# A branch hint as TensorE's first instruction, in place of a visit to a stop inside its loop

## The chip, the cores and the metric

The kernel runs on one core of one Trainium2 chip. The metric is device time in microseconds (us), taken over several executions; lower is better. For every profiled execution there are a page, groups, chains and timelines, and the trace's records of single DMA packets.

Names: PE is TensorE, PEld its weight loads, DVE is VectorE, ACT is ScalarE, POOL is GpSimd, SP is SyncE, which issues nearly all loads. The core has 16 DMA engines, and all loads but that of x are split over all of them (45 loads, each with 16 closing packets of 4 bytes in the trace of the kernel before).

## The reference, cut to what matters

It is one decode step for two sequences: attention over a long cache, a small MLP beside it, and a gate.

```python
xn = layernorm(x)                       # x: 2 x 1 x 512, bf16
q = xn @ wq                             # 512 x 4096: 32 heads of 128
p = softmax(q @ k_cache.T / sqrt(128))  # 8 kv heads, 32768 positions, 2 sequences
s = (p @ v_cache) @ wo                  # 4096 x 512
g = silu(mlp(xn))                       # w3: 512 x 1792, w4: 1792 x 512
return x + s * g
```

The two caches hold 268 of the 280.5 MB that the kernel reads. Each byte is used once, so reading them is most of the work.

## The kernel before: the parts that matter

SP issues the load of wq as its very first instruction, ahead of the three barriers at the start. The other loads follow. TensorE runs a loop of 16 passes, one per (sequence, kv head), after a prologue and before a tail.

The change concerns how TensorE's program itself comes onto the core. The trace of the kernel before has one packet of 16 KB of kind "instruction" among the loads (queue q8, at 4.354 us); its transfer is called the fetch below. The author took it for a later part of TensorE's program; that is an estimate, and e2 and f2 below show what supports it. Before, TensorE was sent at the start through a short stop inside its loop (the "visit", at 0.69 us), so that the packet would be asked for early:

```python
def begin(nc, ins, engine, far):
    ...
    entry.instructions = head + [ins, mybir.InstUnconditionalBranch(target=far, ...)]
    ...                                       # the rest of the entry block goes to "far_back"

first = sp.dma_start(out=wq_t[...], in_=A_wq...)           # 4 MB, first of all loads
begin(nc, first.ins, pe.engine, "far")
...
hint_p, hint_v = pe.mark_branch_hint_location(), dve.mark_branch_hint_location()
...
with pe.Fori(0, NG):                          # 16 passes
    head_sums()
    ...                                       # 64 score matmuls
    nc.br("mid", engines=[pe.engine])         # each pass jumps over the stop:
    with nc.body("far", ...):
        pe.sem_inc(s_far, 1)
        nc.br("far_back", engines=[pe.engine])
    nc.switch_bb("mid")
    ...                                       # 64 p @ v matmuls
early(0); head_sums(); early(1); product(2)   # the tail: s @ wo, part by part as wo lands
...
for i in range(3, len(WO_PARTS)):
    mm = product(i)
...
for eng, hint, reg in ((pe, hint_p, end_p), (dve, hint_v, end_v)):
    eng.br_lt(reg, 1, on_true="fin", on_false="end").branch_hint(hint)   # "the end hint"
```

The softmax here doesn't subtract the row's maximum and nothing guards it: scores larger than these inputs give would overflow.

## Time and profile before

| | before |
|---|---|
| time, median of 3 runs | 654.35 us (654.28 to 654.38) |
| span of the profiled run | 652.9 us |
| read from HBM | 280.50 MB, 430 GB/s over the span |
| PE, DVE busy | 60%, 53% |
| first load issued / next load issued | 0.00 / 1.97 us |
| last wo packet ends | 649.92 us |

The first lines are from the page of the kernel before: the DMA row (busy tenths in 40 slices of the span) and the DMA queues (packets, MB, share of 16 engines' time).

```profile
span 652.9 us, 6540 instructions
...
DMA  9999999999999999999999999999999999989997
...
q1 hardware_dynamic: 6492, 280.50, 99.4%
q8 instruction: 1, 0.02, 0.0%
...
q14 instruction: 1, 0.01, 0.0%
```

DMA is the limit from end to end. The small line to notice is q8: one packet of 16 KB that carries instructions, not data.

The second view is the end of the chain of waits of the kernel before (start us, length us, what).

```profile
613.26 36.95 DMA kbuf<-in_A_wo_dram
650.22 0.04 issue
650.26 0.26 PE bank L643 x4
650.52 0.02 issue
650.54 0.30 DVE sg L667
650.85 0.02 issue
650.87 0.29 DVE out L669
```

The kernel ends less than 3 us after the last piece of wo has landed. So a delay of the DMA engine that delivers last should delay the kernel (in f2 below wo landed 1.1 us earlier, and the span was 1.0 us shorter).

The third view is the start of the timeline of the kernel before (start us, length us, engine, line, operation).

```profile
0.00 0.39 SPq L182 DMA_DIRECT2D kbuf<-in_A_wq_dram  x1
...
1.97 0.33 SPq L225 DMA_DIRECT2D vbuf<-in_B_w_dram  x1
...
2.27 0.27 DVE L254 MEMSET x_bf<- 128x256 uint32 x1 [2.27 <-PEq L187]
```

The packet records show one thing that no view shows. On one DMA engine a packet starts where the packet before it ends (to some nanoseconds: 1655 + 1478 is 3133, and the next starts at 3131), so the records can be chained by engine. On the engine that carries the instruction packet, with start and length in ns:

```
kernel before, one DMA engine:   1655 +1478  wq, 32 KB
                                 3131 +1224  wq
                                 4354  +925  instructions, 16 KB (q8)
                                 5264 +1720  wq
                                 6981 +1219  wq ...
```

The others need about 1213 ns for a wq packet from the fourth on. This engine loses 910 ns to the fetch (5264 - 4354) and 507 ns to the slower packet behind it (1720 - 1213), 1.4 us together. It ends its share of wq at 13.04 us; the next latest ends at 12.11. At the end of the kernel one engine is late again: its last wo packet ends at 649.92 us, the next latest engine's at 648.90. (The 8 KB instruction packet on q14, which ends at 648.98, belongs to no load and isn't counted.) The lag can be followed in between: each load ends on each engine with a packet of 4 bytes, 16 for a load, and in every load up to 640 us the last of the 16 is behind the one before it by 0.93 us at first and 1.02 us from about 290 us on.

### The profile page before, as it was taken

What the parts mean: (1) busy time and instruction counts of PE and PEld (TensorE: products, weight loads), DVE (VectorE), ACT (ScalarE), POOL (GpSimd) and SP (SyncE); (2) the same over time, 40 slices, a digit from 0 to 9 for tenths busy, and PEclk for the clock granted to TensorE, in tenths of its full rate; (3) what the DMA queues carried; (4) which work ended last, traced back from release to release, by engine and by line L of the source; (5) the groups of instructions that cost most, each with busy time, mean ns of one, the idle gap of its engine ahead of it and who ended that gap; (6) DMA issues with size and microseconds to landing.
All of it is one profiled execution on the core that took longest, in us unless ns stands there. A gap on an engine that the chain in (4) does not pass through costs nothing. (4 is left out here: it accounts for less than half of the span.)

```text
span 652.9 us, 6540 instructions
## 1 busy us (share of the span) xinstructions
PE 390.0 (60%) x2406; PEld 156.8 (24%) x2438; DVE 345.8 (53%) x412; ACT 76.8 (12%) x184; POOL 7.7 (1%) x29
## 2 busy tenths in 40 slices
PE   0548195672828658293764829367383945828785
PEld 0213132221313223131221213123121322312332
DVE  3257191744809265391835729174481926539570
ACT  1320102011010200101020010201001020110100
POOL 2100000000000000000000000000000000000000
PEclk9769788786978868698786978878697896869797
DMA  9999999999999999999999999999999999989997
GB/s 384 477 391 452 446 446 401 442 446 450 401 438 446 450 406 434 446 450 401 438 446 450 418 422 450 446 430 410 450 446 442 397 450 446 450 389 448 418 450 292
DMA packets 6506, 280.53 MB, mean 430 GB/s; under 512 B 736, under 2 KB 1000, under 8 KB 1256
## 3 DMA queue, kind: packets, MB, share of 16 engines
q1 hardware_dynamic: 6492, 280.50, 99.4%
q8 instruction: 1, 0.02, 0.0%
q10 hardware_dynamic: 12, 0.01, 0.0%
q14 instruction: 1, 0.01, 0.0%
HBM read 280.50 MB, written 0.00 MB: 430 GB/s over the span
## 5 line engine op out<-in xcount | busy, mean ns | idle before, releaser
L586 PE MATMUL bank<-T,z 128*128 128x512 bf16 x992 | 272.9, 422 | 185.1 <-PEq L46 180.4
L513 DVE STREAM_TRANSPOSE T<-kbuf 128x1024 int32<-128x1024 int32 x256 | 290.6, 1210 | 126.3 <-DVEq L46 126.3
L586 PEld LDWEIGHTS bank<-T,z 128*128 128x128 bf16 x1024 | 97.4, 103 | 347.9 <-issue 270.3
L608 PE MATMUL bank<-vbuf,pt 128*16 128x512 bf16 x1024 | 77.5, 469 | 2.9 <-PEq L46 2.9
L490 ACT ACTIVATE ep<-bank 128x512 bf16<-128x512 f32 x32 | 19.1, 598 | 434.2 <-ACTq L46 434.2
L534 DVE RECIPROCAL rec<-bank 128x1 f32<-128x1 f32 (+1 forms) x17 | 2.9, 169 | 123.1 <-DVEq L46 123.1
L608 PEld LDWEIGHTS bank<-vbuf,pt 128*16 128x16 bf16 x1024 | 28.6, 105 | 43.6 <-issue 28.0
L522 DVE STREAM_TRANSPOSE pt<-ep 128x512 bf16<-128x512 bf16 x32 | 22.8, 714 | 22.1 <-DVEq L46 22.1
L568 PE MATMUL bank<-ob,sel_o 128*128 128x128 f32 x136 | 19.4, 286 | 16.4 <-PEq L46 16.4
L601 PE MATMUL bank<-ones_f,sm 128*128 128x1 f32 x32 | 5.9, 255 | 31.3 <-PEq L46 31.3
L494 ACT COPY ob<-bank 128x512 f32<-128x512 f32 x16 | 9.4, 587 | 107.2 <-ACTq L46 107.2
L568 PEld LDWEIGHTS bank<-ob,sel_o 128*128 128x128 f32 x136 | 16.7, 193 | 21.8 <-issue 21.8
L483 ACT ACT_TABLE_LOAD x16 | 20.5, 1283 | 0.3
L483 ACT COPY z<-qr 32x16 bf16 x64 | 13.0, 203 | 0.7
L601 PEld LDWEIGHTS bank<-ones_f,sm 128*128 128x128 f32 x32 | 5.0, 198 | 32.2 <-issue 32.2
L329 PE MATMUL bank<-ident,xn_bf 17*128 17x17 bf16 x4 | 0.3, 176 | 14.1 <-POOL x L320 14.1
L452 PE MATMUL bank<-vbuf,h_bf 128*32 128x512 bf16 x14 | 4.6, 501 | 6.4 <-DVE h_bf L449 6.4
L563 PE MATMUL bank<-ident 128*1 128x1 bf16 x64 | 8.4, 165 | 0.0
L563 PEld LDWEIGHTS bank<-ident 128*1 128x1 bf16 x64 | 4.0, 82 | 16.2 <-issue 14.4
L542 DVE TENSOR_REDUCE oA<-xm 128x128 f32 x16 | 5.9, 366 | 3.8 <-DVEq L46 3.8
L536 DVE SCALAR_TENSOR_TENSOR xm<-bank,rec,mask 128x128 f32<-128x128 f32 (+1 forms) x17 | 6.0, 351 | 2.5 <-DVEq L46 0.2
L490 ACT ACTIVATION_READ_ACCUMULATOR ep<-bank 128x1 f32 x32 | 6.4, 200 | 0.2
(75 smaller groups left out, 54.9 us busy)
## 6 DMA issues: line engine op xcount, KB each, us to landing
vbuf<-in_A_v_cache_dram SPq DMA_DIRECT2D x4, 4096.0 KB, 29.1
kbuf<-in_A_k_cache_dram SPq DMA_DIRECT2D x2, 4096.0 KB, 22.9
kbuf<-in_A_wq_dram SPq DMA_DIRECT2D x1, 4096.0 KB, 13.5
vbuf<-in_B_w_dram SPq DMA_DIRECT2D x2, 1792.0 KB, 17.7
kbuf<-in_A_wo_dram SPq DMA_DIRECT2D x3, 1024.0 KB, 34.3
kbuf<-in_A_wo_dram SPq DMA_DIRECT2D x1, 512.0 KB, 37.1
kbuf<-in_A_wo_dram SPq DMA_DIRECT2D x1, 256.0 KB, 37.3
kbuf<-in_A_wo_dram SPq DMA_DIRECT2D x2, 128.0 KB, 37.0
```

The costliest lines, as they stand in the source:

```text
L483: i = act.copy(out=z[32 * j:32 * j + 32, :, :, c:c + rep], in_=qr[32 * j:32 * j + 32, :, :, bass.ds(m * rep, rep)],)
L490: act.activation(out=eps_[i][:, :], in_=sc[i][:, :], func=ACT.Exp, scale=inv_sqrt_dh, accum_out=rss[i][:, :]).then_inc(s_e, 1)
L494: act.copy(out=ob[:, :], in_=o[:, :]).then_inc(s_ob, 1)
L513: dve.transpose(out=Ts[(NR * i + r) % T_BUFS][:, :].rearrange("p (b t k) -> p t b k", b=NB, t=RT), in_=kt[:, r * W:(r + 1) * W].rearrange( ...
L522: dve.transpose(out=pts[h][:, :, :].rearrange("p r (t h) -> p t r h", h=rep), in_=eps_[i][:, :].rearrange("p (t r h) -> p t r h", r=NR, h= ...
L536: dve.scalar_tensor_tensor(out=xm[p0:, :, :], in0=oT[p0:, :].rearrange("p (w r) -> p w r", w=WL), scalar=rec[p0:, 0:1], in1=mask[p0:, :].u ...
L542: dve.tensor_reduce(out=dst, in_=xm[p0:, :, :].rearrange("p w r -> p r w"), axis=AX.X, op=ALU.add).then_inc(s_r, 1)
L563: pe.matmul(mark_ps, lhsT=ident[:, 0:1], rhs=ident[:, 0:1], start=True, stop=True).then_inc(sem, 1)
L568: mm = pe.matmul(oT, lhsT=sel_o[:, t, :, :, :].rearrange("p j h w -> p (j h w)"), rhs=ob[:, t * Dh:(t + 1) * Dh], start=(t == 0), stop=(t ...
L586: mm = pe.matmul(sc[i][:, :], lhsT=z[:, nb, e, zc:zc + 128], rhs=Tb[:, nb, :, e], start=(r == 0 and nb == 0 and e == 0), stop=(r == NR - 1 ...
L601: pe.matmul(S, lhsT=sms[1][:, :], rhs=ones_f[:, 0:1], start=True, stop=True)
L608: mm = pe.matmul(o[32 * j:32 * j + VT * rep, :], lhsT=pts[h][:, r, a * VT * rep:(a + 1) * VT * rep], rhs=vt[:, u * VT:(u + 1) * VT, :].rea ...
```

## The change

The intent is to get the packet early without a detour: TensorE need not go to the stop and come back while the first barrier waits for it (TensorE's DRAIN comes at 1.08 us, SP's at 0.455), and the loop loses the jump over the stop. A branch at the top, never taken, has a target in the tail ("late"), and a hint that it will be taken is moved to be TensorE's first instruction.

```diff
-def begin(nc, ins, engine, far):
+def begin(nc, *names):            # now only moves the named instructions to the top
...
-    begin(nc, first.ins, pe.engine, "far")
...
+    ahead = pe.mark_branch_hint_location()
+    top = nc.cur_bb
+    pe.br_lt(end_p, 0, on_true="late", on_false="go").branch_hint(ahead)   # end_p is 0
+    nc.switch_bb("go")
     hint_p, hint_v = pe.mark_branch_hint_location(), dve.mark_branch_hint_location()
+    hints = [i.name for i in top.bb.instructions if isinstance(i, mybir.InstBranchHint)]
+    begin(nc, first.ins.name, *hints)
...
-        nc.br("mid", engines=[pe.engine])
-        with nc.body("far", parent=nc.bb_map["main"], valid_engines=[pe.engine]):
-            pe.sem_inc(s_far, 1)
-            nc.br("far_back", engines=[pe.engine])
-        nc.switch_bb("mid")
...
+    nc.switch_bb("late", parent=top)
     for i in range(3, len(WO_PARTS)):
```

More of the change, by code (lines that the diff above doesn't have):

```diff
@@ L46, in take @@
     eng.wait_ge(sem, n).then_inc(sem, -n)
-def begin(nc, ins, engine, far):
+def begin(nc, *names):
     blocks = nc.m.functions[0].blocks
+    moved = [i for b in blocks for i in b.instructions if i.name in names]
     for b in blocks:
-        b.instructions = [i for i in b.instructions if i.name != ins.name]
-    entry = blocks[0]
-    at = next(n for n, i in enumerate(entry.instructions) if isinstance(i, (mybir.InstMemset, mybir.InstDrain)))
-    head, rest = entry.instructions[:at], entry.instructions[at:]
-    entry.instructions = head + [ins, mybir.InstUnconditionalBranch(target=far, name=f"I-{nc.next_id()}", engine=engine)]
-    with nc.body(f"{far}_back", parent=nc.bb_map[blocks[0].name]):
-        pass
-    *blocks, back = nc.m.functions[0].blocks
-    back.instructions = rest
-    nc.m.functions[0].blocks = blocks[:1] + [back] + blocks[1:]
+        b.instructions = [i for i in b.instructions if i.name not in names]
+    entry = blocks[0].instructions
+    at = next(n for n, i in enumerate(entry) if isinstance(i, (mybir.InstMemset, mybir.InstDrain)))
+    blocks[0].instructions = entry[:at] + moved + entry[at:]
 @with_exitstack
@@ L191 @@
         eng.reg_mov(reg, 0)
+    s_far = nc.alloc_semaphore("s_far")
+    ahead = pe.mark_branch_hint_location()
+    top = nc.cur_bb
+    pe.br_lt(end_p, 0, on_true="late", on_false="go").branch_hint(ahead)
+    nc.switch_bb("go")
     hint_p, hint_v = pe.mark_branch_hint_location(), dve.mark_branch_hint_location()
-    s_far = nc.alloc_semaphore("s_far")
+    hints = [i.name for i in top.bb.instructions if isinstance(i, mybir.InstBranchHint)]
+    begin(nc, first.ins.name, *hints)
     d_x, d_w3, d_w4 = (Count(nc, n) for n in ("d_x", "d_w3", "d_w4"))
```

## The prediction

The sum of the forecast is 654.3 us less 0.7, so 653.6 us. The first step of point 1, on which the 0.7 us rest: the packet, asked for at 0.7 us (the visit) or 2.2 us (the hint) before, would be asked for at about 0.1 to 0.5 us. That a hint is such a request was the assumption. "It" in point 1 is this request; before that, in "It found wq's packets", it is the packet.

> **What bounds the kernel now.** DMA. The page shows the DMA row at 9 tenths in nearly every slice, queue q1 at 99.4% of 16 engines' span, 430 GB/s; PE is 60% busy. The chain that ended last is 5.7% "DMA kbuf<-in_A_wo", 36.95 us of waiting that ends at 650.22, then 0.26 us of PE, 0.30 + 0.29 us of DVE and the output DMA. So the time is 280.5 MB through the DMA engine that finishes last, plus a short tail.
>
> **The engine that finishes last.** I chained the trace's packet records (a packet starts where the one before it on its engine ends). One of the 16 DMA engines is late. It carries a 16,384-byte packet of kind "instruction" (queue q8 on the page: one packet, 0.02 MB), which starts at 4.35 us, takes 0.925 us and is followed by a wq packet of 1.72 us where the others take 1.21: about 1.4 us lost. This engine ends its share of wq at 13.03 us, the next latest at 12.10, most at 11.5 to 11.9. At the end of the kernel 15 engines finish wo by 648.90 and one at 649.91. Every load is split evenly over the engines, so a lag of about 1.0 us from the instruction fetch stays to the end, all on the critical path.
>
> The compiled program before has about 662 TensorE instructions. [...] It found wq's packets (from 1.66 us on this engine) ahead of it.
>
> **What the change does.**
> 1. [...] If it reaches its DMA engine before wq's first packet there (1.66 us), it runs in idle time and the lag shrinks from 1.0 us to about 0.0 to 0.3. If it arrives behind that packet, it costs about what it costs now.
> 2. No visit: TensorE reaches its first DRAIN at about 0.2 us instead of 1.08; the first barrier then waits for SP's DRAIN (0.455), so the three barriers end about 0.5 us earlier (now 1.9 us, timeline). That is off the path: wq is issued at 0.00 before them and keeps the engines busy to 11.5 us.
> 3. The branch over the far block goes (estimate 0.2 us x16 on PE, by the 0.23 us from the branch back to the next instruction). Off the path: PE waits for data in every group.
>
> **Predicted.** 653.6 us, 0.7 us less: about 70% for a gain of 0.5 to 1.0 us, 25% for none, little for worse. Range 653.2 to 654.5. Within 2%: nearly certain.
>
> **What the profile would show.** The q8 packet before or among wq's first packets, at about 1 to 2 us; the same count (one) of them; the engine that carries it no later than the others at the end of wq (about 12.1 us); the last wo packet at about 649.0 instead of 649.91, and landing at about 649.3; first SP issue after the barrier at about 1.4 instead of 1.97 us.
>
> **What would make it wrong.** The fetch still lands behind wq packets (then 654.3); the hint at the first instruction is ignored[...]; other engines' lag (12.10 at wq's end) limits the gain to less; a second fetch appears[...].

## The result, and the profile after

| | before | after |
|---|---|---|
| time, median of 6 runs each | 654.37 us (654.28 to 654.43) | 654.42 us (654.16 to 654.63) |
| span of the profiled run | 652.9 us | 652.8 us |
| next load issued | 1.97 us | 1.45 us |
| instruction packet q8 starts | 4.354 us | 5.578 us |
| latest / next latest engine at the end of wq | 13.04 / 12.11 us | 13.05 / 12.17 us |
| latest / next latest engine at the end of wo | 649.92 / 648.90 us | 649.84 / 648.96 us |

The ratio of the times is 1.0001, with a 95% interval of 0.9988 to 1.0013: no difference. Ratios here and below are the mean time of one kernel's fast runs over that of the other's of the same rounds, so not quite the ratio of the medians quoted beside them.

The page of the changed kernel has the same queues, with the same single instruction packet on q8.

```profile
span 652.8 us, 6524 instructions
...
DMA  9999999999999999999999999999999999999997
...
q1 hardware_dynamic: 6492, 280.50, 99.4%
q8 instruction: 1, 0.02, 0.0%
...
q14 instruction: 1, 0.01, 0.0%
```

The end of its chain of waits has the same form, and the same times within 0.1 us:

```profile
613.16 36.97 DMA kbuf<-in_A_wo_dram
650.13 0.04 issue
650.18 0.26 PE bank L637 x4
650.44 0.02 issue
650.46 0.30 DVE sg L662
650.76 0.02 issue
650.79 0.29 DVE out L664
```

The start of its timeline shows that the barriers do end earlier:

```profile
0.00 0.39 SPq L176 DMA_DIRECT2D kbuf<-in_A_wq_dram  x1
...
1.45 0.33 SPq L224 DMA_DIRECT2D vbuf<-in_B_w_dram  x1
...
1.75 0.27 DVE L253 MEMSET x_bf<- 128x256 uint32 x1 [1.75 <-PEq L181]
```

So the 0.52 us at the start is there, and nothing comes of it. The fetch, which was to come earlier, comes 1.2 us later, although the hint ran at 0.31 us. On its engine it has three wq packets ahead of it and not two:

```
kernel after, one DMA engine:    1343 +1775  wq, 32 KB
                                 3117 +1255  wq
                                 4369 +1213  wq
                                 5578  +931  instructions, 16 KB (q8)
                                 6494 +1712  wq ...
```

### The profile page after: what moved, and what is told of

It is laid out like the page before. It is cut to its first block, busy times and chain, and to the rows that moved or that the text cites. A ratio compares the mean times of both kernels' runs of the same rounds, so it can differ in the third digit from the quotient of the medians.

```text
span 652.8 us, 6524 instructions
## 1 busy us (share of the span) xinstructions
PE 386.2 (59%) x2406; PEld 156.5 (24%) x2438; DVE 346.0 (53%) x412; ACT 76.7 (12%) x184; POOL 7.7 (1%) x29
## 5 line engine op out<-in xcount | busy, mean ns | idle before, releaser
L602 PE MATMUL bank<-vbuf,pt 128*16 128x512 bf16 x1024 | 73.0, 449 | 2.5 <-PEq L46 2.5
```

The source lines that it names most:

```text
L602: mm = pe.matmul(o[32 * j:32 * j + VT * rep, :], lhsT=pts[h][:, r, a * VT * rep:(a + 1) * VT * rep], rhs=vt[:, u * VT:(u + 1) * VT, :].rea ...
```

## The experiments

Two questions are left. What started the fetch, if not the hint at 0.31 us? And does the late engine really set the time, so that a better placed fetch would have paid?

### Who asks for the packet: one part at a time

Four kernels separate the visit, the new hint and the end hint.

```diff
 e1: changed kernel without TensorE's end hint
-        eng.br_lt(reg, 1, on_true="fin", on_false="end").branch_hint(hint)
+    pe.br_lt(end_p, 1, on_true="fin", on_false="end")      # DVE keeps its hint
 e2: changed kernel without the new hint
-    pe.br_lt(end_p, 0, on_true="late", on_false="go").branch_hint(ahead)
+    pe.br_lt(end_p, 0, on_true="late", on_false="go")
 e3: kernel before without TensorE's end hint (same edit as e1)
 e4: no visit, no branch at the top; the end hint moved up to be TensorE's first instruction
```

> The changed kernel with TensorE's second hint (the one for the last branch) taken out. Theory A (the new hint starts the fetch[...]): the q8 packet stays at about 5.6 us. Theory B (the new hint starts no fetch; the second hint at 1.97 us does): no q8 packet in the first microseconds[...]. Time: A 654.4; B 654.4 again if one engine is held up later[...].

> The changed kernel with the new hint taken out, its branch left. Theory B (the second hint starts the fetch): q8 packet at about 5.6 us as in the changed kernel, time 654.4. Theory A: the request now comes 1.7 us later, so the packet moves one or two wq packets later, 6.8 to 8 us, time 654.4.

> The kernel before with TensorE's hint for the last branch taken out, the visit left. If the visit started the fetch in the kernel before (latency 3.66 us from 0.69): q8 packet at about 4.35 us as before. If the hint at 2.17 us did: no packet there, but later. Time 654.4 if the packet stays early.

> No visit and no branch at the top; the hint for the last branch[...] is TensorE's first instruction, at about 0.3 us. If the place of the request decides and a hint for this branch works from there: q8 packet before or just behind the first wq packet of its engine, at 1 to 3.1 us; if before it, the engine's lag at the end of wq falls from 1.4 us over the median to under 0.6 and the time to about 653.5 to 653.8; if behind it, time 654.4. If a hint at the very first instruction is lost whatever its branch: no early packet.

The first table gives times in us. "Late at the end" is by how much the latest DMA engine ends wo after the next latest one; where two engines are late, by how much the earlier of the two ends after the third.

| run | q8 packets start at | late at the end of wo | median (runs) | ratio to before, 95% interval |
|---|---|---|---|---|
| before | 4.35 | 1.02 | 654.33 (7) | |
| e1, new hint, its branch | 5.52 and 68.3 | two engines, 0.90 or more | 654.27 (4) | 0.9998 (0.9981 to 1.0014) |
| e2, branch unhinted, end hint | 66.1 | 0.88 | 654.47 (4) | 1.0003 (0.9987 to 1.002) |
| e3, visit alone | 4.36 and 70.9 | two engines, 1.18 or more | 654.32 (4) | 1.0001 (0.9984 to 1.0018) |
| e4, end hint first | 47.9 | 0.87 | 654.26 (4) | 1.0 (0.9983 to 1.0017) |

Four things follow.

The visit starts the early fetch of the kernel before: e3 has it at the same time without the end hint. Likewise the new hint is needed for the fetch of the changed kernel, since e1 has it and e2, with the same branch unhinted, has not. The end hint starts no early fetch from either place (e2, e4). What it does is suppress a second packet: where it is missing (e1, e3), another 16 KB comes at about 70 us. What was in that packet the trace doesn't tell. Theory B of e1 was wrong: the second hint is not what the changed kernel's fetch comes from. For e2 both theories expected an early packet, and neither got it.

The DMA queues of e3 show the two packets:

```profile
q8 instruction: 2, 0.03, 0.0%
```

In e2 TensorE ran without the packet up to 66.86 us (66.11 + 0.75). The packet came only at 66.08 to 67.00 us, and TensorE stood still in the middle of its p @ v matmuls of the first pass. These are weight loads of e2 in the timeline, with the idle time before them in brackets:

```profile
66.11 0.75 PEld L600 LDWEIGHTS bank<-vbuf,pt 128*16 128x16 bf16 x16 [0.18 <-issue]
68.50 0.10 PEld L600 LDWEIGHTS bank<-vbuf,pt 128*16 128x16 bf16 x4 [1.64 <-issue]
```

The same 64 loads ran through in the kernel before:

```profile
63.23 3.13 PEld L608 LDWEIGHTS bank<-vbuf,pt 128*16 128x16 bf16 x64
```

So what the packet carries seems to begin inside the loop, at the last four of the p @ v matmuls. (That the wait was for the packet is read from the times: it ended at 67.00 us, and TensorE went on at 68.50.) What the visit and the hint were there for was this one stall of 1.64 us. It cost nothing in the time (654.47 us in e2, ratio 1.0003), so TensorE is not what the kernel waits for at that point. In e4 there was no stall either: with neither visit nor new hint the packet came at 47.9 us, and the 64 p @ v matmuls of the first pass ran through from 62.07 us; why it came so much sooner there than in e2 was not tried. The simplest of these kernels is as fast as any.

Last, the date of the packet makes no difference. At 4.4, 5.5, 48 or 66 us it costs one engine about the same, and the times agree. The 4-byte packets that end each load show the step within one run: in e4 the latest engine is 0.11 us behind the next at the end of wq and of the load that ends at 40 us, and 1.00 us behind at the load that ends at 50 us, just after the packet at 47.9; in e2 it is 0.27 us up to 59 us and 0.88 us at 80 us, with the packet at 66.1 between them. Two packets, in e1 and e3, made two engines late and the time no longer (654.27 and 654.32 us, against 654.33): the latest one counts.

### Is the late engine what the time is waiting for?

Run f2 is to take the packet away. TensorE's program is cut to 418 instructions (about 662 before) by leaving out matmuls: half of the score terms, half of the p @ v terms, half of the q product, most of the early parts of s @ wo. The loads are untouched. That so short a program brings no packet was the guess; the page below bears it out.

```diff
 f2, on the changed kernel, without the hinted branch at the top
-                    for e in range(2):
+                    for e in range(1):                      # score matmuls
-            for u in range(NU):
+            for u in [*range(NU // 4), *range(NU - NU // 4, NU)]:   # p @ v
-        for k in range(DK):
+        for k in (0, DK - 1):                               # q
-    for r in range(r0, r1):
+    for r in (range(r0, r0 + NQ) if r0 == 0 else range(r1 - NQ, r1)):   # early()
-        for r in range(r0, r1):
+        for r in range(r0, min(r1, r0 + 2)):                # product()
```

> TensorE's program cut to 418 instructions[...] (matmuls left out, wrong result on purpose; the loads are the same). Theory L: no q8 packet, the 16 DMA engines finish wo within 0.4 us of each other, the last wo lands about 1 us earlier, time 653.4. Rival R (fetch costs nothing in the time): 654.3. [...]

It measured 653.73 us (5 runs, 653.22 to 653.90) against 654.32 for the kernel before in the same rounds (9 runs, 654.18 to 655.29). The ratio is 0.9987 (0.9973 to 1.0001). By the interval that is just short of clear, but all five runs lie below all nine. The forecast of 653.4 was 0.3 us too low, and rival R's 654.3 is above all five. The comparison with the reference passed all the same, at its tolerance; a kernel that leaves out half of its terms is still no kernel to use.

The DMA lines of f2's page have no q8 line at all:

```profile
span 651.9 us, 4378 instructions
...
q1 hardware_dynamic: 6492, 280.50, 99.5%
q10 hardware_dynamic: 12, 0.01, 0.0%
q14 instruction: 1, 0.01, 0.0%
```

And in its chain of waits the last wo lands 1.1 us earlier than before (649.12 against 650.22):

```profile
612.11 37.01 DMA kbuf<-in_A_wo_dram
649.12 0.04 issue
649.16 0.32 PE bank L632 x4
```

In the packet records the two latest engines end wo at 648.79 and 648.71, where before they ended at 649.92 and 648.90. The latest engine has come down to the others by 1.1 us, and the next latest has moved by only 0.2. All 16 end within 0.6 us (0.4 was forecast).

TensorE also had less work in f2, and the last wo was issued 1.15 us earlier (612.11 against 613.26), so a rival is that this, and not the missing packet, brought the gain. The packet records speak against it. At the end of wq the latest engine of f2 is at 12.00 us, and that of the kernel before at 13.04: 1.04 of the 1.13 us are there before TensorE's first matmul, at 12.94 us in f2. From there to the end the latest engine of f2 is never more than 0.08 us behind the next, in load after load. So the theory stands: one engine, delayed by one instruction packet, held the whole kernel up by about 0.6 us by the medians of the times, 0.85 by the ratio, 0.9 by the medians of the spans (652.1 against 653.0) and 1.0 by the spans of the profiled runs. Why the medians give less than the lag is open.

### Can the fetch be put before wq?

If a fetch on an idle engine costs nothing, it would pay to have it before wq's packets. Five kernels tried, by moving the branch closer to the hint, by issuing wq later, or both.

```diff
 f1: changed kernel, wq issued after the first barrier (0.74 us); the hint stays first
-    begin(nc, first.ins.name, *hints)
+    begin(nc, *hints)
 g1: register move, hint and branch are TensorE's first three instructions (branch at 0.51 us)
 g2: g1, and wq issued after the first barrier (0.92 us)
 h1: hint at 0.41 us, branch right after the first barrier (0.88 us)
 h2: h1's order (branch at 0.85 us), and wq issued after the third barrier (1.57 us)
```

> The changed kernel, but wq is issued after the three barriers (about 1.45 us) and not first; the hint stays TensorE's first instruction. All DMA work then starts 1.45 us later. The q8 packet, asked for at 0.31 us, should find its engine idle. Theory L (the engine that carries the fetch sets the end): its lag of 1.0 us is gone, so the time is 654.4 + 1.45 - 1.0 = about 654.8. Rival R (the lag is hidden by something else; all the DMA start counts): 655.8. If the fetch is still behind wq's packets (the hint starts nothing until its branch is reached): 655.8 with the lag in the packet records.

> The changed kernel with the hinted branch itself moved up: register move, hint and not-taken branch are TensorE's first three instructions, before the first barrier; wq first as before. Theory T (the hint only says what the branch will do; the fetch starts when the sequencer comes to that branch): the branch comes at about 0.45 us and not 1.81, so the q8 packet moves one or two wq packets up, from 5.6 to 4.4 us or less (3.1, or before the first wq packet). Rival H (the hint itself starts the fetch, or the second hint at about 1.9 us does): it stays at 5.5 to 5.6. Time: 654.4 if behind a wq packet, 653.5 if before the first.

> The same, with wq issued after the first barrier (about 0.74 us, so that its first packets start at 1.7 to 3.0 us). T: the fetch is asked for some 2 us before the first wq packet of its engine, finds it idle, and the q8 packet is at 1.5 to 2.5 us; the lag of 1.0 us at the end is gone and the time is 654.4 + 0.6 (as measured for wq late alone) - 1.0 = 654.0. H: packet at about 6.3 us as with wq late alone, 655.0.

> The changed kernel with the hint at about 0.4 us and its not-taken branch right after the first barrier, at about 0.9 us (in the changed kernel 1.81, in the run with the branch at entry 0.51, which fetched nothing early). Theory T2 (the fetch starts when the sequencer comes to a branch whose hint was taken in some time before): q8 packet at about 4.4 us, one wq packet earlier than in the changed kernel. If the lead of 0.4 us is still too short: no early packet, one at 45 to 70 us. Rival H2 (the hint starts the fetch some microseconds later by itself, and a branch too soon only cancels it): 5.5 us as in the changed kernel. Time 654.4 in each case, one engine about 1.0 us late at the end.

> The same start, but wq issued only after the third barrier, at about 1.5 us, so that its packets start at 2.5 to 3.8 us. T2: the fetch, started at about 0.9 us, finds its engine idle: q8 packet at 1.5 to 2.6 us, no engine late at the end, time 654.4 + 1.4 - 1.0 = 654.8. H2: packet behind wq packets (6 us or later), one engine late, 655.8.

Times are in us; the medians of the kernel before in the same rounds were 654.32 (f1), 654.70 (g1, g2) and 654.45 (h1, h2), of 9 runs each.

| run | hint / branch | first wq packet | q8 packet | span | median of 5 | ratio, 95% interval |
|---|---|---|---|---|---|---|
| after | 0.31 / 1.81 | 1.04 | 5.58 | 652.8 | 654.42 (6 runs) | 1.0001 (0.9988 to 1.0013) |
| f1 | 0.32 / 2.28 | 1.75 | 6.36 | 653.6 | 654.95 | 1.0009 (0.9995 to 1.0023) |
| g1 | 0.41 / 0.51 | 1.02 | 55.3 | 653.0 | 654.29 | 0.9999 (0.9985 to 1.0013) |
| g2 | 0.41 / 0.52 | 1.93 | 53.8 | 653.9 | 655.23 | 1.0012 (0.9998 to 1.0026) |
| h1 | 0.41 / 0.88 | 1.02 | 54.5 | 654.1 | 654.51 | 1.0004 (0.999 to 1.0018) |
| h2 | 0.42 / 0.85 | 2.59 | 60.4 | 654.4 | 655.74 | 1.0025 (1.0011 to 1.0039) |

(The profiled execution of h1 was one of the slower ones, 655.42 us, with an engine 1.8 us late; three of the five runs lie at 654.2 to 654.5.)

The expectation of f1 took wq to be issued at 1.45 us; the edit moved it only to 0.74, and of its three cases the last came true, with the lag (1.04 us) in the packet records. In f1 the engine that carried the fetch got its first wq packet at 2.70 us, so for 2.4 us after the hint it had no data to move. The fetch still came behind three wq packets. A request that was there soon after the hint would have had an idle engine. So no request that the hint may have started reached the engine within 2.4 us.

In all runs with the new hint and an early fetch the packet came 3.7 to 4.1 us after the not-taken branch (5.52 - 1.80 in e1, 5.58 - 1.81 in the changed kernel, 6.36 - 2.28 in f1). That suggested that the fetch starts at the branch. It doesn't show it: on a busy engine a packet started where the one before it ended, here every 1.2 us, and the 5.2 to 6.0 us from the hint to the packet lie within one such step too. But with the branch 0.1 us behind the hint (g1, g2), or 0.4 to 0.5 us (h1, h2), no early fetch came at all; theory T of g1 and T2 of h1 predicted 4.4 us or sooner, and rivals H and H2 5.5. None of these was right as stated; what came true is the case that h1's expectation named besides, a lead still too short and a packet at 45 to 70 us (54.5). What is shown is only this: the early fetch needs the hint (e1 against e2), it came in all kernels whose branch ran about 1.5 us or more behind the hint, and in none of the four with 0.5 us or less. The lead is not isolated: in these four the register move that the branch tests also stands before the hint, where in the others it stands between hint and branch, and there are fewer barriers between hint and branch (none or one, not three). Whether the branch starts the fetch and the hint needs time to take hold, or the hint starts it late and a quick branch cancels it, stays open. The lead between 0.5 and 1.5 us was not tried.

None of the five got the packet before wq. Delaying wq costs nearly all of its delay: first packets later by 0.7, 0.9 and 1.6 us than in the kernel before (1.01) went with spans longer by 0.7, 1.0 and 1.5 us than its 652.9 (f1, g2, h2). How long a delay would let the fetch through was not found; the longest of these, 1.6 us, already costs more than the lag of 1.0 us.

### Can the late engine be relieved instead?

```diff
 f3, f4: changed kernel; wo part 3 (rows of 4 KB) as two transfers, cut = 120 or 56
-        d_wo[i].after(sp.dma_start(out=wo3[:, g, w], in_=wos[:, g, w]), 16)
+        for rows in ((slice(0, cut), slice(cut, 128)) if i == 3 else (slice(0, 128),)):
+            d_wo[i].after(sp.dma_start(out=wo3[rows, g, w], in_=wos[rows, g, w]), 16)
```

The author reckoned with 15 engines for the 120 rows and 8 for the 8 rows of f3, and with 14 and 12 engines in f4. One engine (called the 16th in the text) was to get nothing of this part in f3; in f4 two (15 and 16) were to get nothing, two (13 and 14) less than before and twelve more. The numbers of engines agree with the packets counted below; which engines get the rows no run shows.

> The changed kernel with wo part 3 (rows of 4 KB) loaded as rows 0 to 119 and rows 120 to 127. [...] If the fetch is carried by the 16th engine: its lag is gone and by theory L the time is 653.4 to 653.6; by rival R 654.4. If by another engine: it keeps its lag or has 0.15 us more, 654.4 to 654.6.

> The same part split into rows 0 to 55 (14 engines, 4 rows each) and 56 to 127 (12 engines, 6 rows each)[...]. If the fetch is on 15 or 16: time 653.7 (limit then 0.3 us more on the others); on 13 or 14: 653.9; on 1 to 12: 654.7.

Both lost: 656.32 us (ratio 1.0026, 1.0013 to 1.004) and 655.98 us (1.0024, 1.001 to 1.0038), against 654.32. The count of packets agrees with the numbers of engines reckoned with: the packets under 512 B, which include one 4-byte completion per engine, rose from 736 to 743 and 746, and 15 + 8 and 14 + 12 engines in place of 16 make 7 and 10 more. But the packets near the end became slow. The 4 KB packets took 246 ns on average in f3, and 159 in the kernel before; the 2 KB packets 131 and 84. Why was not tried. In both, one engine still ended wo long after the next, by 1.7 us in f3 (651.86 against 650.12) and 1.1 us in f4 (651.52 against 650.42), so if engines were spared as reckoned, the one with the fetch is probably not among them. Which one it is these runs don't tell. They are a miss, and the uneven transfers at the end cost more here (2.0 and 1.7 us by the medians) than the lag of 1.0 us that they were to spare.

No correct version was found that beats both kernels.

## Why the prediction was right or wrong

- What bounds the kernel: right. It is the DMA engine that ends last, and f2 measured its lag: without the instruction packet the last wo landed 1.1 us earlier, and 1.04 us of that was there at the end of wq.
- The late engine and its cause: right, by f2, by e3, where two packets made two engines late, and by e2 and e4, where the lag begins with the packet. The estimate of about 1.0 us on the critical path was of the right size.
- The visit, not the hint at 2.17 us, started the old fetch: left open in the prediction, settled by e3.
- The packet is asked for at about 0.1 to 0.5 us instead of 0.7 or 2.2 (the assumption), and so may reach "its DMA engine before wq's first packet there (1.66 us)": this step failed, and with it the expected gain of 0.7 us. It left some 1.3 us between the hint and the packet. The hint did run at 0.31 us, but the packet started at 5.58 us, 5.3 us after it and 1.2 us later than before. In f1 the engine had no wq packet for 2.4 us after the hint, and the fetch still came behind wq. So it is refuted that the hint brings a request to its engine within 1.3 us. Whether that request takes long, is made late, or comes from the branch at 1.81 us, is open. The trace of the kernel before had a warning: if the visit at 0.69 us was what asked (e3 shows it), its fetch had 1.0 us before wq's first packet on that engine, and missed it too.
- The time: 654.42 us lies inside the stated range of 653.2 to 654.5, but only because the range took in the case of no gain, which was given 25%. "The fetch still lands behind wq packets (then 654.3)", given as a way to be wrong, is what happened. The profile that was forecast did not come: q8 at 5.58 us and not 1 to 2, its engine at 13.05 us at the end of wq and not 12.1, the last wo packet at 649.84 us and not 649.0.
- "If it arrives behind that packet, it costs about what it costs now": right. It left its engine late by 0.9 to 1.0 us at the end, whether at 4.4, 5.6, 48 or 66 us (the kernel before, the changed kernel, e4, e2).
- No visit: the next load was expected at 1.4 us and was issued at 1.45. That it gains nothing was right too.
- The jump over the stop in the loop is gone and gains nothing: right as far as the whole tells. The time is the same, and so is the end of the chain of waits, to 0.1 us.
- A second fetch, named as a way to be wrong: this did not happen. The end hint had the opposite effect, one packet fewer (e1 and e3 against the two kernels).

## What to carry to other kernels

When DMA is the limit and every load is split evenly, look for the one engine that ends last: a single extra packet of 16 KB made this kernel 0.6 to 1.0 us longer, and no view of mean busy time shows it. The hint was no request that was met at once here: the transfer came 5.3 us after it. Look in the trace for the transfer that it was meant to start, before its place in the program is tuned. And moving such a cost within a stretch that is full from end to end gained nothing here; only leaving it out did.
